# Threshold attention with a SwiGLU layer: the last group's final feed-forward blocks done chunk by chunk, and the two last copies exchanged between VectorE and ScalarE

## The chip, the cores and the metric

The kernel runs on one core of a Trainium2 chip. The metric is device time in microseconds (us). Times are medians of several executions; the profile is one execution, so its span can differ from the median. The kernel before took 564.16 us (564.16 to 564.22, three runs).

## The reference, cut to what matters

```python
def _attn_ref(q, k, v, tau):                 # 8 batches, 8 heads, 576 rows, head size 64
    scores = scale * np.matmul(q, k.transpose(0, 1, 3, 2))
    thresh = np.max(scores, axis=-1, keepdims=True) - tau
    scores = np.where(scores >= thresh, scores, -1000000000.0)
    ...                                      # softmax
    return np.matmul(attn, v)

def _moe_ref(x, w_gate, w_val, w_out, rms_g):  # x: 4608 x 512, feed-forward width 1536
    xn = x / rms * rms_g
    g = xn @ w_gate
    silu = g * (1.0 / (1.0 + np.exp(-g)))
    val = xn @ w_val
    return (silu * val @ w_out).astype(np.float32)
```

Only the last product, `(silu * val) @ w_out`, for the last 256 of 4608 rows, is touched by the change.

## The kernel before

The kernel builds a list of operations, each with an engine, an estimated cost, a priority and the operations that it depends on; a greedy simulation then orders them. Rows go through the feed-forward layer in groups of chunks of 128 rows. The last group has two chunks. The width of 1536 makes twelve blocks of 128. For the last group the output product is "streamed": each block's product is added to the chunk's sums in PSUM as soon as the block's gated values (`hf`) are there.

```python
        if streamed:
            acc = None
            for fc, (hi, m_) in enumerate(hs):          # twelve blocks
                def omm(o, fc=fc, hi=hi, first=acc):
                    for j in range(len(parts)):         # two chunks
                        nc.tensor.matmul(ring[(first or o).slot[j]], hf[hi][:, 128 * j:128 * (j + 1)], wo[:, fc],
                                         start=(fc == 0), stop=(fc == NFC - 1))
                ...
        for j, (ci, _) in enumerate(parts):
            ...
            late = streamed and j % 2
            def ev(o, ...):                             # the copy of a chunk's sums, PSUM to SBUF
                if late:
                    nc.vector.tensor_scalar(out=osb[oi], in0=ring[mo.slot[at]], scalar1=0.5, scalar2=None, op0=ALU.mult)
                else:
                    nc.scalar.activation(out=osb[oi], in_=ring[mo.slot[at]], func=AF.Copy, scale=0.5)
            def store(o, ...):
                    ...
                    (nc.scalar if late else nc.sync).dma_start(out=dst, in_=osb[oi])
```

So chunk 0 is copied by ScalarE and stored from SyncE's queue; chunk 1 is copied by VectorE and stored from ScalarE's queue.

Of the kernel before, what the change touches and what calls it, by code (L numbers as in the profile page):

```python
# [15 lines left out]
COST = dict(  # L16
    s_main=932.0, s_virt=900.0, tr_qk=530.0, tr4=230.0, tr_full=440.0, av_main=310.0, av_virt=480.0, ffn4=216.0, warm=3500.0,
    ttr=690.0, evac_qk=600.0, evac_half=380.0, evac_kt=350.0, prelu=700.0, exp2=1250.0, exp1=690.0, exp0=690.0,
    mask_d=750.0, mask_g=1740.0, take_g=1300.0, trw=510.0, evac_w=450.0, evac_wp=900.0, rz=180.0, xmul=420.0, sq=800.0, xn=720.0,
    pool_tiny=270.0, pool_mean=800.0, pool_dma=850.0, cast_v=650.0, cast_vt=420.0, cast_w=720.0,  # L20
    sp=420.0, sp_v=600.0, sp_w=600.0, sp_tr=1300.0, sp_qk=680.0, sp_tl=630.0,
)
# [105 lines left out]
def kernel(  # L128
# [18 lines left out]
    NFC = DFF // 128  # L147
# [10 lines left out]
    def ps(name, n):  # L158
        return psum.tile([128, n], FP32, tag=name, name=name)
# [49 lines left out]
    ring = [ps(f"ring{i}", 512) for i in range(4)]  # L209
# [11 lines left out]
    def add(eng, cost, prio, deps, fn, **kw):  # L221
        o = Op(eng, cost, prio, deps, fn, **kw)
        ops.append(o)
        return o
# [543 lines left out]
    sl_use, th_use, osb_use = {}, {}, {}  # L768
# [3 lines left out]
    def emit_ffn(slot, parts, ready_step, pace, streamed):  # L772

        n = 128 * len(parts)
        push1 = EPUSH[1] if parts[0][0] < EPUSH[0] else PUSH[1]
        nu = NFC + len(parts)
        st = max(clock[0], ready_step)
        dt = pace * n / 512.0 / nu
        clock[0] = st + pace * n / 512.0
        xops = [t for _, t in parts]  # L780
        hs = []
        mm = 4 * COST["ffn4"] * n / 512.0
        el = (n + 90) / 0.96
        uses = []
        for fc in range(NFC):
            pr = st + dt * fc
            fs = slice(128 * fc, 128 * (fc + 1))
            i = count["gv"] % NT_
            count["gv"] += 1
            hi = count["hf"] % NHF  # L790
            count["hf"] += 1

            def gmm(o, fs=fs):
                for d in range(4):
                    nc.tensor.matmul(ring[o.slot[0]][:, 0:n], wg[d][:, fs], xnT[slot][:, d, 0:n],  # L795
                                     start=(d == 0), stop=(d == 3))

            def vmm(o, fs=fs):
                for d in range(4):
                    nc.tensor.matmul(ring[o.slot[0]][:, 0:n], wv[d][:, fs], xnT[slot][:, d, 0:n],  # L800
                                     start=(d == 0), stop=(d == 3))

            g = add("PE", mm, pr, count["v"] + xops + w_done[fc // 4] + hf_use.get(hi, []), gmm, ring="R")
            vv = add("PE", mm, pr + 0.01, [g] + xops + hf_use.get(hi, []), vmm, ring="R")

            count["v"] = [vv]

            def tanh(o, i=i, g=g):
                nc.scalar.activation(out=th[i][:, 0:n], in_=ring[g.slot[0]][:, 0:n], func=AF.Tanh, scale=0.5)  # L809

            def silu(o, i=i, g=g):
                nc.vector.scalar_tensor_tensor(  # L812
                    out=sl[i][:, 0:n], in0=th[i][:, 0:n], scalar=1.0, in1=ring[g.slot[0]][:, 0:n],
                    op0=ALU.add, op1=ALU.mult)

            def gate(o, i=i, vv=vv, hi=hi):
                nc.vector.tensor_tensor(out=hf[hi][:, 0:n], in0=ring[vv.slot[0]][:, 0:n], in1=sl[i][:, 0:n], op=ALU.mult)  # L817

            t = add("ACT", el, pr - PUSH[0], [g, th_use.get(i)], tanh)
            s_ = add("DVE", el + 40, pr - push1, [t, sl_use.get(i)], silu, frees=(g, 0))  # L820
            th_use[i] = s_
            m_ = add("DVE", el, pr - push1, [s_, vv], gate, frees=(vv, 0))
            sl_use[i] = m_
            hs.append((hi, m_))
            uses += [g, vv]
        xnT_use[slot] = uses
        outs = []
        if streamed:

            acc = None  # L830
            for fc, (hi, m_) in enumerate(hs):
                def omm(o, fc=fc, hi=hi, first=acc):
                    for j in range(len(parts)):
                        nc.tensor.matmul(ring[(first or o).slot[j]], hf[hi][:, 128 * j:128 * (j + 1)], wo[:, fc],  # L834
                                         start=(fc == 0), stop=(fc == NFC - 1))

                mo = add("PE", len(parts) * COST["ffn4"], st + dt * (fc + OUT_LAG), [m_] + wo_ld + outs[-1:], omm,
                         ring=None if acc else "R", nring=len(parts))
                if not acc:

                    acc, mo.pick = mo, ACC
                outs.append(mo)
                hf_use[hi] = [mo]
        for j, (ci, _) in enumerate(parts):
            kind, b, c = chunks[ci]
            pr = st + dt * (NFC + j)
            oi = count["o"] % 2
            count["o"] += 1
            if streamed:
                mo, at = acc, j  # L850
            else:
                mo, at = None, 0
                for lo in range(0, NFC, OUT_PART):
                    def omm(o, j=j, lo=lo, first=mo):
                        for fc in range(lo, lo + OUT_PART):
                            nc.tensor.matmul(ring[(first or o).slot[0]], hf[hs[fc][0]][:, 128 * j:128 * (j + 1)],  # L856
                                             wo[:, fc], start=(fc == 0), stop=(fc == NFC - 1))

                    need = [m_ for _, m_ in hs[0:lo + OUT_PART]] + wo_ld + (outs[-1:] if mo else [])
                    o = add("PE", OUT_PART * COST["ffn4"], pr - (1.0 if mo else 0.0), need, omm, ring=None if mo else "R")  # L860
                    mo = mo or o
                    outs.append(o)

            late = streamed and j % 2

            def ev(o, oi=oi, mo=mo, at=at, late=late):
                if late:
                    nc.vector.tensor_scalar(out=osb[oi], in0=ring[mo.slot[at]], scalar1=0.5, scalar2=None, op0=ALU.mult)
                else:
                    nc.scalar.activation(out=osb[oi], in_=ring[mo.slot[at]], func=AF.Copy, scale=0.5)  # L870

            def store(o, oi=oi, kind=kind, b=b, c=c, late=late):
                if kind == "m":
                    dst = out[b * S:b * S + MAIN].rearrange("(si sc) d -> si sc d", sc=4)[:, c]
                    (nc.scalar if late else nc.sync).dma_start(out=dst, in_=osb[oi])
                else:
                    for e in range(2):
                        r0 = (2 * b + e) * S + MAIN
                        nc.sync.dma_start(out=out[r0:r0 + TAIL], in_=osb[oi][64 * e:64 * e + 64])

            e = add("DVE" if late else "ACT", 690.0 if late else 620.0, pr - PUSH[0], [outs[-1], osb_use.get(oi)], ev,
                    frees=(mo, at))
            late = late and kind == "m"
            osb_use[oi] = add("ACT" if late else "SP", COST["sp"] if kind == "m" else 1100.0, pr, [e], store,
                              dma=DMA_NS['out'])
        if not streamed:
            for hi, _ in hs:
                hf_use[hi] = list(outs)
# [23 lines left out]
    for c in range(DFF // 512):  # L912
        for d in range(0, 4, 2):
            for w_dram, w_sb in ((moe_w_gate, wg), (moe_w_val, wv)):
                slot = n // 2 % len(stage)
                pr = W_FROM + W_STEP * n
# [17 lines left out]
    wo_ld = []  # L934
    wo_src = moe_w_out.rearrange("(fc p) d -> p fc d", p=128)
    for j in range(4):
        o = add("POOL", COST["pool_dma"], W_FROM + W_STEP * n + j + WO_AT, [], lambda o, j=j: nc.gpsimd.dma_start(
            out=wo[:, 3 * j:3 * j + 3], in_=wo_src[:, 3 * j:3 * j + 3]), dma=DMA_NS['wo'], bulk=True)
# [3 lines left out]
    for s, (ci, p) in enumerate(steps):  # L942
# [5 lines left out]
        if p == NP - 1:  # L948
            gi, j = place[ci]
            xt_op[ci] = emit_x(ci, s, gi % NXT, 128 * j)  # L950
            if ci in last_of:
                g = groups[last_of[ci]]
                emit_ffn(last_of[ci] % NXT, [(ci_of[x], xt_op[ci_of[x]]) for x in g], s + (ELAG if place[ci][0] < NELAG else LAG), PACE,
                         last_of[ci] >= len(groups) - STREAMED)
# [19 lines left out]


PACE = 13.0
ACC = (4, 6)
OPENS = ((4,), (6,))
NHF = 12
# [7 lines left out]
OUT_LAG = 5.0  # L987
# [6 lines left out]
PUSH = (40.0, 0.0)  # L994
# [54 lines left out]
```

## Time and profile before

| what | value | where it is read |
|---|---|---|
| median time | 564.16 us | three runs |
| span of the profiled run | 562.9 us | first line of the page |
| TensorE busy | 98% | first part of the page |
| last matmul ends | 558.85 us | timeline, start plus duration of the last row of matmuls |
| last store issued, landed | 559.61, 562.0 us | timeline, and 2.4 us from issue to landing in the DMA view |

TensorE is busy for 98% of the span, and its last matmul ends at 558.85. Four microseconds follow: a copy, a store's issue, its landing and a closing. The lines themselves are in the prediction. One number I call the **tail**: the span less the end of the last matmul, 562.9 - (556.53 + 2.32) = 4.05 us.

### The profile page before, as it was taken

The numbers are of one execution on the slowest core, as the hardware profiler recorded it, in microseconds if no ns is written. First come the engines' busy times: TensorE is split into PE (matmuls) and PEld (weight loads), VectorE is DVE, ScalarE is ACT, GpSimd is POOL, SyncE is SP. The second block draws the span as 40 slices with busy tenths as digits, with TensorE's granted clock in tenths as the row PEclk, the third lists the DMA queues.
The fourth block names the chain that finished last, engine by engine and source line by source line (L and its number), as shares of the span: only waits on it lengthen the run. The fifth ranks groups of instructions, "written<-read, shape, count | busy, mean of one in ns | idle before, by whom it ended". The sixth has DMA issues, their size and how long they took to land.

```text
span 562.9 us, 15217 instructions
## 1 busy us (share of the span) xinstructions
PE 553.0 (98%) x5768; PEld 315.7 (56%) x5768; DVE 425.5 (76%) x1091; ACT 459.9 (82%) x741; POOL 322.5 (57%) x462
## 2 busy tenths in 40 slices
PE   8899999999999999999999999999999999999997
PEld 4656766757767555545555455545555444444674
DVE  4889987869968589658885889578966886596354
ACT  5999998998989788879888997888989988885332
POOL 2378946985767456665667666666666664551000
PEclk9999999999999999999999999999999999999999
DMA  8999999979986498889887799988898544662210
GB/s 189 259 283 271 159 191 192 193 145 187 202 184 115 111 178 156 181 161 186 151 175 174 122 168 179 181 179 157 171 189 178 116 95 92 151 95 52 85 39 37
DMA packets 270025, 89.08 MB, mean 158 GB/s; under 512 B 252544, under 2 KB 262272, under 8 KB 269952
## 3 DMA queue, kind: packets, MB, share of 16 engines
q1 hardware_dynamic: 267168, 86.02, 75.8%
q0 software_dynamic: 1600, 1.57, 1.8%
q8 instruction: 45, 0.74, 0.6%
q10 hardware_dynamic: 1184, 0.52, 0.3%
q14 instruction: 28, 0.23, 0.2%
HBM read 37.75 MB, written 9.44 MB: 84 GB/s over the span
## 4 chain that ended last, share of the span: by engine, by line
PE 94%; DVE 2%; ACT 1%; DMA 1%; issue 1%; POOL 0%; SPq 0%; DVEq 0%
PE s_ps L569 30%; PE ring L795 17%; PE ring L800 16%; PE ring L856 15%; PE ring L700 6%; PE ring L304 2%; PE ring L696 2%; DVE ssb L592 1%; PE ring L662 1%; PE s_ps L800 1%; PE s_ps L834 1%; PE s_ps L856 1%; DMA stage<-in_q_dram 1%; PE ring L365 1%; PE s_ps L795 0%
## 5 line engine op out<-in xcount | busy, mean ns | idle before, releaser
L592 DVE CUSTOM_DVE_ANT_0 ssb<-s_ps,zrow 128x576 f32<-128x576 f32 x288 | 207.1, 752 | 64.4 <-PE s_ps L569 46.5
L610 ACT ACTIVATE ssb<-ssb,nth 128x576 f32<-128x576 f32 x224 | 166.1, 767 | 27.5 <-POOL nth L599 27.1
L569 PE MATMUL s_ps<-qkt 64*64 64x288 f32 (+1 forms) x1792 | 165.9, 417 | 1.5 <-DVE mx L592 1.5
L643 POOL TENSOR_SCALAR wsb<-ssb,nth 128x576 f16<-128x576 f32 x64 | 110.5, 1726 | 9.7 <-DMA wt<-wsb 3.2
L795 PE MATMUL ring<-xnT,wg 128*128 128x256 f16 (+1 forms) x564 | 114.4, 325 | 0.3 <-DVE xsb L718 0.3
L569 PEld LDWEIGHTS s_ps<-qkt 64*64 64x64 f32 (+1 forms) x1792 | 78.1, 140 | 62.5 <-DVE mx L592 15.5
L800 PE MATMUL ring<-xnT,wv 128*128 128x512 f16 (+1 forms) x528 | 110.4, 331 | 0.0
L599 POOL TENSOR_SCALAR nth<-mx 128x2 f32<-128x2 f32 x144 | 31.7, 220 | 128.1 <-DVE mx L592 118.0
L812 DVE SCALAR_TENSOR_TENSOR sl<-th,ring 128x256 f32<-128x256 f32 (+1 forms) x141 | 77.0, 546 | 30.9 <-ACT th L809 29.6
L617 ACT ACTIVATE wsb<-ssb 128x1152 f16<-128x1152 f32 x80 | 93.0, 1162 | 4.3 <-DMA wt<-wsb 2.2
L809 ACT ACTIVATE th<-ring 128x256 f32<-128x256 f32 (+1 forms) x141 | 67.5, 480 | 29.7 <-PE ring L795 24.7
L856 PE MATMUL ring<-wo,hf 128*128 128x512 f16 x384 | 90.0, 380 | 0.0
L648 POOL TENSOR_TENSOR wsb<-wsb,esb 128x576 f16<-128x576 f16 x64 | 81.8, 1279 | 10.3 <-ACT esb L629 6.0
L817 DVE TENSOR_TENSOR hf<-ring,sl 128x512 f16<-128x512 f32 (+1 forms) x132 | 74.9, 567 | 9.3 <-PE ring L800 0.5
L800 PEld LDWEIGHTS <-wv 128*128 128x128 f16 x576 | 52.2, 98 | 44.5 <-issue 14.2
L795 PEld LDWEIGHTS <-wg 128*128 128x128 f16 x576 | 52.0, 98 | 42.2 <-issue 12.2
L856 PEld LDWEIGHTS <-hf 128*128 128x128 f16 x408 | 37.3, 98 | 47.0 <-issue 7.0
L629 ACT ACTIVATE esb<-ssb,nth 128x576 f16<-128x576 f32 x64 | 49.2, 769 | 6.1 <-POOL nth L599 5.8
L700 PE MATMUL ring<-va,wt 128*128 128x65 f16 (+1 forms) x1264 | 53.0, 193 | 0.0
L700 PEld LDWEIGHTS <-wt 128*128 128x128 f16 (+1 forms) x1280 | 48.8, 100 | 3.8 <-issue 0.7
L614 ACT ACTIVATE wsb<-ssb 128x576 f16<-128x576 f32 x64 | 43.6, 681 | 1.6
L696 PE MATMUL ring<-va,wt 128*128 128x130 f16 (+1 forms) x158 | 35.2, 227 | 0.6 <-ACT qTv L473 0.6
(68 smaller groups left out, 442.3 us busy)
## 6 DMA issues: line engine op xcount, KB each, us to landing
vst<-in_v_dram SPq DMA_DIRECT2D x32, 256.0 KB, 3.7
qkn<-in_k_dram SPq DMA_DIRECT2D x31, 256.0 KB, 3.8
out_dram<-osb SPq DMA_DIRECT2D x31, 256.0 KB, 2.8
qkn<-in_q_dram SPq DMA_DIRECT2D x28, 256.0 KB, 4.3
stage<-in_moe_w_gate_dram SPq DMA_DIRECT2D x6, 512.0 KB, 5.9
stage<-in_moe_w_val_dram SPq DMA_DIRECT2D x6, 512.0 KB, 6.5
wt<-wsb SPq DMA_TRANSPOSE x128, 3.3
wo<-in_moe_w_out_dram POOLq DMA_DIRECT2D x4, 384.0 KB, 6.6
```

Source lines behind the costliest of these rows:

```text
L569: nc.tensor.matmul(s_ps[h][rows, ROW_AT + n * part:ROW_AT + n * part + n], lhs(hs), kT[i][p][h][hs, n * part:n * part + n], start=True, st ...
L592: nc.vector.tensor_tensor_reduce(out=ssb[a][:, h], in0=s_ps[h][:, ROW_AT:ROW_AT + S], in1=zrow, scale=-1.0 / 8.0, scalar=3.0e38, op0=ALU.a ...
L610: nc.scalar.activation(out=ssb[a][:, h], in_=ssb[a][:, h], func=PRELU, scale=-1.0, bias=nth[m][:, h:h + 1], **PRELU_KW)
L617: nc.scalar.activation(out=wsb[s % NW], in_=ssb[a], func=AF.Exp)
L643: nc.gpsimd.tensor_scalar(out=wsb[s % NW][:, h], in0=ssb[a][:, h], scalar1=nth[m][:, h:h + 1], scalar2=None, op0=ALU.is_le)
L648: nc.gpsimd.tensor_tensor(out=wsb[s % NW][:, h], in0=wsb[s % NW][:, h], in1=esb[es], op=ALU.mult)
L700: nc.tensor.matmul(ring[o.slot[0]][rs, at:at + D + 1], w[:, 5 * h + j, rs], va[vi][:, p, 2 * j + h], start=False, stop=(h == 1 and j == 3))
L795: nc.tensor.matmul(ring[o.slot[0]][:, 0:n], wg[d][:, fs], xnT[slot][:, d, 0:n], start=(d == 0), stop=(d == 3))
L800: nc.tensor.matmul(ring[o.slot[0]][:, 0:n], wv[d][:, fs], xnT[slot][:, d, 0:n], start=(d == 0), stop=(d == 3))
L812: nc.vector.scalar_tensor_tensor(out=sl[i][:, 0:n], in0=th[i][:, 0:n], scalar=1.0, in1=ring[g.slot[0]][:, 0:n], op0=ALU.add, op1=ALU.mult)
L817: nc.vector.tensor_tensor(out=hf[hi][:, 0:n], in0=ring[vv.slot[0]][:, 0:n], in1=sl[i][:, 0:n], op=ALU.mult)
L856: nc.tensor.matmul(ring[(first or o).slot[0]], hf[hs[fc][0]][:, 128 * j:128 * (j + 1)], wo[:, fc], start=(fc == 0), stop=(fc == NFC - 1))
```

## The change

The intent is to have chunk 0's sums complete earlier, so that its copy and store are out of the way when chunk 1's come, and to let chunk 1's copy and store both be done by ScalarE.

```diff
-            for fc, (hi, m_) in enumerate(hs):
-                def omm(o, fc=fc, hi=hi, first=acc):
-                    for j in range(len(parts)):
+            turns = [(fc, tuple(range(len(parts)))) for fc in range(NFC - BY_ROW)]
+            turns += [(fc, (j,)) for j in range(len(parts)) for fc in range(NFC - BY_ROW, NFC)]
+            last_out = {}
+            for n_, (fc, js) in enumerate(turns):
+                hi, m_ = hs[fc]
+                def omm(o, fc=fc, hi=hi, js=js, first=acc):
+                    for j in js:
                         nc.tensor.matmul(...)
 ...
-                if late:
+                if streamed and not late:
                     nc.vector.tensor_scalar(...)
                 else:
                     nc.scalar.activation(...)
 ...
-            e = add("DVE" if late else "ACT", ..., [outs[-1], osb_use.get(oi)], ev,
+            on_dve = streamed and not late
+            e = add("DVE" if on_dve else "ACT", ..., [last_out[j] if streamed else outs[-1], osb_use.get(oi)], ev,
 ...
+BY_ROW = 4
```

The queues of the stores are not changed: chunk 0 by SyncE, chunk 1 by ScalarE.

More of the change, by code (lines that the diff above doesn't have):

```diff
@@ L830, in emit_ffn @@
             acc = None
-            for fc, (hi, m_) in enumerate(hs):
-                def omm(o, fc=fc, hi=hi, first=acc):
-                    for j in range(len(parts)):
+            turns = [(fc, tuple(range(len(parts)))) for fc in range(NFC - BY_ROW)]
[5 more added lines that the diff above has]
+                    for j in js:
                         nc.tensor.matmul(ring[(first or o).slot[j]], hf[hi][:, 128 * j:128 * (j + 1)], wo[:, fc],
                                          start=(fc == 0), stop=(fc == NFC - 1))
-                mo = add("PE", len(parts) * COST["ffn4"], st + dt * (fc + OUT_LAG), [m_] + wo_ld + outs[-1:], omm,
-                         ring=None if acc else "R", nring=len(parts))
+                late = len(js) == 1 and js[0]
+                mo = add("PE", len(js) * COST["ffn4"], st + dt * (fc + OUT_LAG + (NFC if late else 0)),
+                         [m_] + wo_ld + outs[-1:], omm, ring=None if acc else "R", nring=len(parts))
                 if not acc:
@@ L842, in emit_ffn @@
                 outs.append(mo)
+                for j in js:
+                    last_out[j] = mo
                 hf_use[hi] = [mo]
@@ L879, in store @@
                         nc.sync.dma_start(out=out[r0:r0 + TAIL], in_=osb[oi][64 * e:64 * e + 64])
-            e = add("DVE" if late else "ACT", 690.0 if late else 620.0, pr - PUSH[0], [outs[-1], osb_use.get(oi)], ev,
+            on_dve = streamed and not late
+            e = add("DVE" if on_dve else "ACT", 690.0 if on_dve else 620.0, pr - PUSH[0],
+                    [last_out[j] if streamed else outs[-1], osb_use.get(oi)], ev,
                     frees=(mo, at))
```

## The prediction

> **What bounds the kernel now.** I read the page's header and engine shares first, then the timeline of the last microseconds, since the change touches only the last group's end, then the chain of waits there, and last the DMA view of the same stretch.
>
> ```profile
> span 562.9 us, 15217 instructions
> ...
> PE 553.0 (98%) x5768; PEld 315.7 (56%) x5768; DVE 425.5 (76%) x1091; ACT 459.9 (82%) x741; POOL 322.5 (57%) x462
> ```
>
> TensorE is busy 98% of the span, and the other engines have room. Whatever does not shorten TensorE's stream can gain only in what follows its last matmul. The timeline (start, duration, engine, line, operation) shows that end:
>
> ```profile
> 556.09 0.60 PE L800 MATMUL ring<-xnT,wv 128*128 128x256 f16 x4
> 556.28 0.42 DVE L812 SCALAR_TENSOR_TENSOR sl<-th,ring 128x256 f32<-128x256 f32 x1 [0.36 <-ACT th L809]
> 556.42 1.93 PEld L834 LDWEIGHTS <-hf 128*128 128x128 f16 x10
> 556.53 2.32 PE L834 MATMUL s_ps<-wo,hf 128*128 128x512 f16 x10
> 556.80 0.42 DVE L817 TENSOR_TENSOR hf<-ring,sl 128x256 f16<-128x256 f32 x1
> 558.67 0.60 ACT L870 ACTIVATE osb<-s_ps 128x512 f32<-128x512 f32 x1 [2.43 <-PE s_ps L834]
> 558.89 0.69 DVE L868 TENSOR_SCALAR osb<-s_ps 128x512 f32<-128x512 f32 x1 [1.66 <-PE s_ps L834]
> 559.29 0.33 SPq L875 DMA_DIRECT2D out_dram<-osb  x1
> 559.61 0.36 ACTq L875 DMA_DIRECT2D out_dram<-osb  x1
> ```
>
> The reader is to see three things. The ten last matmuls (blocks 7 to 11 for two chunks) are evenly spaced: (2.32 - 0.379 that one takes) / 9 = 0.216 us. ScalarE copies chunk 0 from 558.67, after the last but one matmul; VectorE copies chunk 1 from 558.89, 0.04 after the last matmul ended (556.53 + 2.32 = 558.85). And the two stores go out 0.32 us apart, so they are on the DMA engines together. The chain that ended last says the same of the last store's origin:
>
> ```profile
> 556.69 2.17 PE s_ps L834 x10
> 558.87 0.02 issue
> 558.89 0.69 DVE osb L868
> ```
>
> The end is matmuls, VectorE's copy of chunk 1, its store, the landing, and the program's closing. The DMA view of 559 to 563 us (40 slices of 0.1 us) shows what the store costs:
>
> ```profile
> DMA  0000000000059999999999999200000000000000
> GB/s 0 0 0 0 0 0 0 0 0 0 0 205 389 430 389 369 389 348 431 389 369 369 389 369 348 62 0 0 0 0 0 0 0 0 0 0 0 0 0 0
> ...
> out_dram<-osb SPq DMA_DIRECT2D x1, 256.0 KB, 2.2
> out_dram<-osb ACTq DMA_DIRECT2D x1, 256.0 KB, 2.4
> ```
>
> From about 560.1 to 561.55 all 16 engines are full: two stores of 256 KB back to back. ScalarE's store lands 2.4 us after its issue, at 559.61 + 2.4 = 562.0; the remaining 0.9 us to 562.9 are the closing, which the change leaves alone. The same kind of store when alone, 541 to 544 us (slices of 0.075 us, issue at 541.26):
>
> ```profile
> DMA  0000000000000036999999963000000000000000
> ```
>
> Its data run from about 542.05 to 542.9, so they begin 0.8 after the issue and take 0.83. The view of the output tensor from 535 to 550 us gives the landing of such lone stores:
>
> ```profile
> DMA to landing us min/median/max: 2.1/2.1/2.1
> ```
>
> So the last store is late by 2.4 - 2.1 = 0.3 us. A second way: alone, it would have had its last byte at 559.61 + 0.8 + 0.83 = 561.25, but the engines fall idle near 561.55, again 0.3.
>
> **What the Trainium skill says.** "DMA: Bandwidth & Descriptors", section "Issuing engines are not separate DMA queues", states that DMAs started by scalar, sync or gpsimd all run on the same 16 DMA engines and interleave. The trace agrees: issued from two queues, 0.52 MB moves at one store's rate, some 390 GB/s. "Perfetto Trace Analysis", section "DMA Instruction — HWDGE (DVE, Sync)", says that the profiled length of the DMA instruction is only the issue. The trace agrees: 0.33 us of issue against 2.1 to landing. "PSUM — Partial Sum Buffer", section "Summary: rules for kernel authors", says to aim at a different bank when PSUM is read while a matmul runs. The two chunks' sums lie in different `s_ps` tiles, and before already copies chunk 0 at 558.67 while the last matmul (558.47 to 558.85) writes the other.
>
> **The change, part by part.**
>
> Order of matmuls. Blocks 0 to 7 stay pairwise; blocks 8 to 11 are then done for chunk 0 (four matmuls) and next for chunk 1 (four). The count stays 24, each with its own weight load, so TensorE's work is the same. Four matmuls in a row into one bank instead of alternating ones should cost nothing: the group before it has runs of 12 into one bank at 2.75 us (L856 in the timeline), and 11 x 0.216 + 0.379 = 2.755. The greedy ordering of the program sees the same candidates up to block 7, so everything before is unchanged. TensorE: 0.
>
> Need for block 11. Chunk 0's block 11 becomes the sixth of the ten instead of the ninth. It would start at 556.53 + 5 x 0.216 = 557.61, its weight load some 0.11 earlier, at 557.50. VectorE writes block 11's `hf` until 556.80 + 0.42 = 557.22. That leaves about 0.28 us. No stall: 0.
>
> Chunk 0's way out. Its last matmul ends at 557.61 + 0.38 = 557.99, four slots of 0.216 before the very last. VectorE starts its copy at 558.03 (0.04 later, as before), ends at 558.72, and SyncE issues the store near 558.75 instead of 559.29: 0.54 earlier. Data run from 559.55 to 560.4. This is off the end's path by itself; it only gets out of the way.
>
> Chunk 1's way out, the path. The last matmul still ends at 558.85, and the copy starts at 558.89. It is ScalarE's now: 0.597 instead of 0.690 (the L870 and L868 rows), ended at 559.49 instead of 559.58: 0.09 gained. The issue follows on ScalarE's own queue. Before, the step from VectorE's end to ScalarE's issue was 0.03, so removing the change of engine can give at most this; and since a write must be complete before a DMA reads it, I expect that a wait of some such size stays. I count 0. The issue is at 559.52. Its data would start at 560.32, with the first store's data ending at 560.4: an overlap of under 0.1 us instead of 0.5. I take the lone store's 2.1: landing at 561.6 instead of 562.0.
>
> Sum: 0.09 (shorter copy) + 0.3 to 0.36 (no queueing behind the other store) = about 0.42 us. 564.16 - 0.42 = 563.74, which is 0.07%.
>
> **The rivals.**
>
> The transfer is late for its queue, not for its neighbour. If a store issued by ScalarE takes 2.4 us even alone, only the copy's 0.09 is gained: 564.07. For it: the profile has no lone store from that queue, and its issue is 0.36 long against 0.33. Against it: the engines are full all through the 1.45 us, and the delay is what sharing would give.
>
> TensorE waits for block 11. If the semaphore from VectorE takes longer than the 0.28 us of slack, every later matmul moves by the difference. Even 0.2 us of it would only halve the gain: 563.95. Against it: elsewhere in this timeline consumers start 0.04 us after producers.
>
> The wait after ScalarE's own copy costs more than one between engines. ScalarE's queue may have to drain before it issues. If this cost 0.3 us, the time would be 564.04. The profile of before has no copy and store on the one queue, so it says nothing against it but that such steps cost 0.03 elsewhere.
>
> The whole order shifts. The order comes from a greedy simulation of all operations; a change early in the list could move microseconds either way. But no earlier operation's cost, priority or dependencies change. I give it about 1%.
>
> **Range and chances.** The central value has all of the removed queueing and the faster copy. If every rival but the last came true together, I would be at about 564.2; if the issue also gains the 0.03 and the landing gets shorter, at 563.6. The runs of before spread by 0.06. So 563.4 to 564.2. The gain or loss would have to be 11 us for a verdict other than the same, which nothing in the last 4 us can give.
>
> **What would show it.** In the changed profile: the L834 row still ten matmuls spaced 0.216 and ending 2.32 after it starts; VectorE's copy at about 558.0 and ScalarE's at 558.9; SyncE's issue 0.5 us earlier; ScalarE's issue within 0.05 after its copy; the DMA view with two humps that hardly overlap; ScalarE's landing 2.1 instead of 2.4; span near 562.5. A gap in the ten matmuls would show the second rival, a landing still of 2.4 with the engines idle before it the first, and a gap between copy and issue the third. A different start of the last group (the first block at 548.7) would show that the order shifted and prove me wrong.

## More of the kernel before

As spans are given to a tenth, a tail is good to about 0.05. The tail has an advantage over the time: what loads do at the start of a run does not enter it. Each tail is read from one profiled execution.

## The result, and the profile after

The changed kernel took 563.88 us (563.40 to 564.06, four runs), the kernel before 564.19 in the same rounds (564.16 to 564.23). The ratio is 0.9993, with a 95% interval from 0.9976 to 1.001. Ratios here are the mean time of one kernel's fast runs over that of the other's in the same rounds, so not quite the ratio of the medians. The time lies in the predicted range, 0.14 us above the predicted 563.74. The interval includes 1, so these times do not show a gain.

The timeline of the changed kernel's end (start us, duration us, engine, line, operation, and in brackets the idle time before and its releaser):

```profile
555.93 2.32 PE L840 MATMUL s_ps<-wo,hf 128*128 128x512 f16 x10
556.21 0.42 DVE L817 TENSOR_TENSOR hf<-ring,sl 128x256 f16<-128x256 f32 x1
557.43 0.69 DVE L877 TENSOR_SCALAR osb<-s_ps 128x512 f32<-128x512 f32 x1 [0.80 <-PE s_ps L840]
558.15 0.33 SPq L884 DMA_DIRECT2D out_dram<-osb  x1
558.29 0.60 ACT L879 ACTIVATE osb<-s_ps 128x512 f32<-128x512 f32 x1 [2.64 <-PE s_ps L840]
558.92 0.36 ACTq L884 DMA_DIRECT2D out_dram<-osb  x1
```

The last matmul ends at 555.93 + 2.32 = 558.25. The ten matmuls take as long as before. Chunk 0's copy now begins 0.82 before that end, and its store is issued 0.10 before it; before, the store was issued 559.29 - 558.85 = 0.44 after it. ScalarE's copy ends at 558.89 and its store is issued 0.03 later. The end of the chain of waits has ScalarE's copy where VectorE's stood:

```profile
556.10 2.17 PE s_ps L840 x10
558.27 0.02 issue
558.29 0.60 ACT osb L879
```

The DMA view of the changed kernel from 558 to 562 us, again in slices of 0.1 us, with the size and the time from issue to landing of each store:

```profile
DMA  0000000003899999629999996100000000000000
GB/s 0 0 0 0 0 0 0 0 0 123 307 369 369 410 430 369 205 82 369 369 369 369 369 451 246 41 0 0 0 0 0 0 0 0 0 0 0 0 0 0
...
out_dram<-osb SPq DMA_DIRECT2D x1, 256.0 KB, 2.1
out_dram<-osb ACTq DMA_DIRECT2D x1, 256.0 KB, 2.1
```

There are two humps with a dip between them instead of one block, and ScalarE's store lands after 2.1 us instead of 2.4. The tail is 561.9 - 558.25 = 3.65 us, 0.40 less than before; the prediction's sum was 0.42.

The span has shrunk by 1.0, though, from 562.9 to 561.9, and 0.6 of this is already there at the last group's first output block (548.71 before, 548.11 after). This part lies before the changed matmuls. In the timeline of the first 24 us, TensorE waits for a load of q in the profiled run of before:

```profile
23.21 0.52 PE L365 MATMUL ring<-id,qkn 128*128 128x128 f32 x3 [0.72 <-DMA qkn<-in_q_dram]
```

In the profiled run of the changed kernel the same transposes start without that wait:

```profile
22.52 0.55 PE L365 MATMUL ring<-id,qkn 128*128 128x128 f32 x3
```

From there on TensorE runs 0.6 ahead to the last group. Whether this differs between kernels or only between executions is a question for the experiments.

### The profile page after: what moved, and what is told of

It reads as the page before. It is cut to its first block, busy times and chain, and to the rows that moved or that the text cites. A ratio compares the mean times of both kernels' runs of the same rounds, so it can differ in the third digit from the quotient of the medians.

```text
span 561.9 us, 15217 instructions
## 1 busy us (share of the span) xinstructions
PE 554.2 (99%) x5768; PEld 316.4 (56%) x5768; DVE 425.3 (76%) x1091; ACT 460.0 (82%) x741; POOL 322.4 (57%) x462
## 4 chain that ended last, share of the span: by engine, by line
PE 95%; DVE 2%; POOL 1%; ACT 1%; issue 1%; DVEq 0%; POOLq 0%
PE s_ps L569 29%; PE ring L795 17%; PE ring L800 16%; PE ring L865 15%; PE ring L700 6%; PE ring L304 2%; PE ring L696 2%; DVE ssb L592 1%; PE ring L662 1%; PE ring L365 1%; PE s_ps L800 1%; PE s_ps L840 1%; PE s_ps L865 1%; PE s_ps L262 1%; PE s_ps L795 0%
```

## The experiments

My theory has two terms: chunk 1's store no longer queues behind chunk 0's on the DMA engines (about 0.3 us), and chunk 1's copy is ScalarE's 0.60 instead of VectorE's 0.69. A first rival says that the gain comes from having copy and store on one engine; a second that ScalarE's queue was slow in itself; a third that the lead of 0.6 belongs to the change. All runs but `small_first`, which is wrong, gave correct results. The tails of all runs are in one table at the end of this section. All times compared here count as fast runs (granted clock 0.996 to 1.0); a run that was executed once has only its tail used.

### changed_again: the changed kernel once more

No edit.

> The changed kernel once more, for the spread. I call tail the span less the end of the last matmul (start plus duration of the last row of matmuls): 562.9 - (556.53 + 2.32) = 4.05 us before, 561.9 - (555.93 + 2.32) = 3.65 changed. Theory (the gain is 0.35 of freed DMA engines plus 0.09 of a shorter copy, all of it after the last matmul): tail 3.65 again, and the time about 0.4 below before's. Rival (the 0.6 us by which the profile already leads at the last group's first block is a gain of the change too): 1.0 below before's, and the lead there in this profile as well.

Measured: 564.26 us median of six (563.97 to 565.93) against 564.86 for the kernel before (564.28 to 565.83, eleven runs of the kernel before in this set); ratio 0.9992, interval 0.998 to 1.0004. The tail is 562.1 - (556.08 + 2.32) = 3.70. The tail agrees with the theory. So does the ratio, 0.0008 of 564.86 being 0.45 us, but its interval includes 1. The lead at the last group was in this profile too (its last matmul ends at 558.40), so by the profile alone the rival could still stand. The times do not rule it out either: 1.0 us below would be a ratio of 0.9982, just inside the interval. The next run settles it.

### order_only: only the matmuls' order

```diff
-                if streamed and not late:
+                if late:
                     nc.vector.tensor_scalar(...)
-            on_dve = streamed and not late
+            on_dve = late
```

> Only the order of the matmuls is changed; chunk 0 is copied by ScalarE and stored by SyncE, chunk 1 copied by VectorE and stored by ScalarE, as before. Theory: the stores no longer meet, landing 2.1 instead of 2.4; VectorE's copy is 0.09 longer than ScalarE's, so tail 3.65 + 0.09 = 3.75, about 0.3 below before. Rival (the gain comes from copy and store being on one engine): tail near 4.05.

Measured: 564.34 us (564.01 to 565.84, five runs), ratio 0.9994, interval 0.9982 to 1.0006. The profiled run was a long one, with a span of 563.7:

```profile
557.60 2.32 PE L840 MATMUL s_ps<-wo,hf 128*128 128x512 f16 x10
```

Its last matmul ends at 557.60 + 2.32 = 559.92, 1.7 us later than in the changed kernel, though the edit leaves TensorE's program as it is. Of this, 1.0 us is one wait for the same load of q, at 22.6 us. So the order of the matmuls does not bring the lead with it, and the third rival falls. The kernel before alone spreads over 1.5 us in this set (564.28 to 565.83), which fits with a difference between executions. The tail is 563.7 - 559.92 = 3.78, as the theory has it. ScalarE's landing is 2.1:

```profile
out_dram<-osb SPq DMA_DIRECT2D x1, 256.0 KB, 2.1
out_dram<-osb ACTq DMA_DIRECT2D x1, 256.0 KB, 2.1
```

Copy and store are here on different engines, as before, and most of the gain is there. The first rival falls.

### swap_only: only the copies' engines

```diff
-BY_ROW = 4
+BY_ROW = 0
```

> Only the copies' engines are swapped; the matmuls stay pairwise as before. Theory: chunk 0's copy by VectorE ends 0.09 later, so its store starts 0.09 later; both stores together keep the DMA engines full, and the last landing is set by the first store's start plus both transfers: tail 4.05 + 0.09 = 4.15, a little slower than before, although the last copy is shorter. Rival (one engine for copy and store, with a shorter copy, is worth something of its own): tail 3.95 or less.

Measured: 565.26 us (564.58 to 565.48, five runs), ratio 1.0001, interval 0.9989 to 1.0013. The matmuls' row is

```profile
556.80 2.32 PE L840 MATMUL s_ps<-wo,hf 128*128 128x512 f16 x10
```

and the tail is 563.3 - (556.80 + 2.32) = 4.18. The chunk 1 copy is the short one, and yet the tail is longer than before. The DMA view of 559 to 563 us:

```profile
DMA  0000000000000009999999999999600000000000
...
out_dram<-osb SPq DMA_DIRECT2D x1, 256.0 KB, 2.2
out_dram<-osb ACTq DMA_DIRECT2D x1, 256.0 KB, 2.6
```

ScalarE's store is issued earlier after the last matmul than before (559.79 - 559.12 = 0.67 against 0.76) but lands 2.6 after its issue instead of 2.4: it pays with queueing what it won with the copy. The last byte is set by when the first store starts, and this one starts 0.1 later, since VectorE copies chunk 0 more slowly. So the two terms of the change do not add: without the order the swap is worth less than nothing, with it about 0.1 by the rounded tails (3.78 - 3.65 or 3.70), 0.06 by the unrounded ones of the last table.

### small_first: the store ahead made small

The kernel before, with one store cut to 16 rows of 128:

```diff
-                    (nc.scalar if late else nc.sync).dma_start(out=dst, in_=osb[oi])
+                    if streamed and not late:
+                        nc.sync.dma_start(out=dst[0:16], in_=osb[oi][0:16])
+                    else:
+                        (nc.scalar if late else nc.sync).dma_start(out=dst, in_=osb[oi])
```

> The kernel before, but chunk 0's last store writes 16 of its 128 rows (the result is wrong on purpose). Matmuls, copies and queues are as before; only the transfer ahead of ScalarE's store shrinks to an eighth. Theory (ScalarE's store waits for DMA engines that chunk 0's store keeps full): its landing falls from 2.4 to 2.1 us and the tail from 4.05 to 3.70. Rival (a store issued by ScalarE takes 2.4 by itself in this order): landing 2.4, tail 4.05.

Measured: one run, 564.72 us. The DMA view of the end:

```profile
out_dram<-osb ACTq DMA_DIRECT2D x1, 256.0 KB, 2.1
out_dram<-osb SPq DMA_DIRECT2D x1, 32.0 KB, 1.6
```

Order, copies and queues are those of before; only the bytes ahead are gone, and ScalarE's landing falls to 2.1. The second rival falls: the queue is not slow in itself. The tail is 562.6 - (556.49 + 2.32) = 3.79, where I had 3.70. By the rounded numbers it fell by 0.26 instead of 0.35 (0.32 by the unrounded ones); the issue is as late as before (559.58 - 558.81 = 0.77), so the whole fall is the landing's.

### two_blocks: half the separation

```diff
-BY_ROW = 4
+BY_ROW = 2
```

> The changed kernel with the last two blocks done chunk by chunk instead of four. Chunk 0's sums are ready 2 x 0.216 later, so its store is issued at 0.33 us after the last matmul instead of 0.11 before it. From swap_only and before, two stores that meet land 2.75 us after the first issue (before: issue 559.29, last landing 559.61 + 2.4 = 562.0). Theory: landing at 0.33 + 2.75 = 3.08 after the last matmul, against 2.77 in the changed kernel: tail 3.65 + 0.3 = 3.95. Rival (any chunk-by-chunk order is enough): 3.65.

Measured: one run, 564.23 us. Tail 562.1 - (555.78 + 2.32) = 4.00, and the landings in the DMA view:

```profile
out_dram<-osb SPq DMA_DIRECT2D x1, 256.0 KB, 2.3
out_dram<-osb ACTq DMA_DIRECT2D x1, 256.0 KB, 2.4
```

With two blocks the stores still meet, and most of the gain is gone. This is the dose to go with the effect: 4.18 with none, 4.00 with two, 3.65 to 3.70 with four. A store occupies the engines for 0.83 us; four blocks put the two issues 558.92 - 558.15 = 0.77 apart, which is almost that. Two put them 558.76 - 558.42 = 0.34 apart.

### both_on_sync: copy and store on different engines

```diff
-                    (nc.scalar if late else nc.sync).dma_start(out=dst, in_=osb[oi])
+                    nc.sync.dma_start(out=dst, in_=osb[oi])
```

and the store's operation is given to SyncE in the list as well.

> The changed kernel, but chunk 1's store is issued by SyncE too, so ScalarE's copy hands over to another engine's queue. The stores are now issued 0.8 us apart, longer than the 0.33 that an issue takes. Theory (one engine for copy and store is worth nothing): issue within 0.05 of ScalarE's copy, tail 3.65 within 0.05. Rival (the hand-over costs): tail 3.75 or more.

Measured: one run, 564.27 us; tail 562.1 - (556.16 + 2.32) = 3.62. SyncE issues the store at 559.14, 0.02 after ScalarE's copy ends (558.52 + 0.60). The hand-over from ScalarE to SyncE costs nothing that can be seen. The part of the change's words that sounds most like a gain, one engine's queue for copy and store, is not where the gain is.

### halves_five and halves_six: two versions meant to beat the change

Chunk 1's copy is cut into two halves of 256 columns, and the first half is stored while the second is copied; chunk 0 is got out of the way still earlier.

```diff
+                elif late:
+                    for i, queue in enumerate((nc.sync, nc.scalar)):
+                        cols = slice(256 * i, 256 * i + 256)
+                        nc.scalar.activation(out=osh[i], in_=ring[mo.slot[at]][:, cols], func=AF.Copy, scale=0.5)
+                        queue.dma_start(out=...[:, c_, cols], in_=osh[i])
 ...
-BY_ROW = 4
+BY_ROW = 5          # halves_six: 6
```

`osh` are two idle buffers of the attention part.

> A version meant to beat the changed kernel: the last five blocks chunk by chunk, and chunk 1's copy in two halves of 256 columns on ScalarE, the first stored by SyncE and the second by ScalarE. Chunk 0's store is issued at 0.32 before the last matmul's end. The second half's copy should end at about 0.04 + 0.6 to 0.7, its store carries 128 KB, 0.41 of transfer instead of 0.83. Theory: landing at the later of 0.70 + 0.03 + 0.83 + 0.41 + 0.42 = 2.4 and -0.32 + 2.75 = 2.43 (engines full from the first store on): tail 3.3, time some 0.35 below the changed kernel. Rival (a store's landing is a fixed 2.1 whatever its size, or rows of 1 KB move slower): tail 3.7. TensorE: block 11 is needed 0.216 earlier, with 0.06 of slack left: the ten matmuls should still take 2.32.

> As halves_five with six blocks chunk by chunk. Chunk 1's block 6 can no longer fill the wait before the last value matmuls, so up to 0.2 us is lost ahead of the end and eleven matmuls are left after it; chunk 0's store is issued at 0.54 before the end. Theory: tail 3.3 as set by the second half's own path (2.4), the same as halves_five, and the first-to-last time of the L840 matmuls up to 0.2 longer than its 10.1: so no better than halves_five, perhaps 0.2 worse. Rival (the first store still sets the landing): tail 3.1.

Measured: halves_five 564.36 us (564.25 to 564.94, five runs) against 564.52 for before, ratio 0.9999, interval 0.9985 to 1.0013. halves_six 565.05 us (564.72 to 565.22), ratio 1.0007, interval 0.9994 to 1.0019. The tails are 562.1 - (555.73 + 2.32) = 4.05 and 563.0 - (556.31 + 2.66) = 4.03. Both of my forecasts of 3.3 missed by 0.7, and the rivals (3.7 and 3.1) missed too. The stores of halves_five in the DMA view:

```profile
out_dram<-osb SPq DMA_DIRECT2D x1, 256.0 KB, 2.1
out_dram<-ssb SPq DMA_DIRECT2D x1, 128.0 KB, 1.9
out_dram<-ssb ACTq DMA_DIRECT2D x1, 128.0 KB, 2.0
```

The last one is issued at 558.78 and lands at about 560.8, which is 2.7 us after the last matmul (558.05) where I had 2.4. The changed kernel has 558.92 + 2.1 - 558.25 = 2.77. So two things have to be explained: the landing hardly came forward, and what follows the landing grew from 3.65 - 2.77 = 0.9 to 4.05 - 2.7 = 1.3. For the second I looked at the closing's line, that is, the last instructions of SyncE's queue. In halves_five (operation, count, shortest/median/longest ns, first and last start):

```profile
L1066 SPq EVENT_SEMAPHORE  x10: 17/28/28, 560.8 to 562.1; - x10
L1066 SPq DRAIN  x3: 7/7/7, 561.3 to 561.6; - x3
```

In the changed kernel:

```profile
L1056 SPq EVENT_SEMAPHORE  x9: 17/28/28, 558.5 to 561.9; - x9
L1056 SPq DRAIN  x3: 7/7/7, 561.1 to 561.4; - x3
```

In halves_five not one of the closing waits is passed before 560.8, the moment of the landing; they then follow each other for half a microsecond before the first drain. In the changed kernel they begin at 558.5 and the drain comes within 0.1 of the landing at 558.92 + 2.1 = 561.0. The closing waits for the semaphores of the DMA transfers one after the other, in a fixed order. A third store moves every later transfer on by one in the turn of semaphores, and the last store got the one that is waited for first. That was the new theory, not yet shown, and the next three runs test it.

halves_six shows besides where the chunk-by-chunk order starts to cost. Its timeline:

```profile
556.31 2.66 PE L841 MATMUL s_ps<-wo,hf 128*128 128x512 f16 x11
...
557.28 1.19 PEld L841 LDWEIGHTS <-hf 128*128 128x128 f16 x7 [0.44 <-DVE hf L818]
```

Eleven matmuls would take 10 x 0.216 + 0.379 = 2.54; they take 2.66, as the weight load waits for block 11's `hf`. With five blocks the load also waits (0.22), but the ten matmuls still take 2.32. Four blocks show no such wait. From the first to the last output matmul halves_six takes 10.27 us against 10.14 in the changed kernel, within the 0.2 that I had allowed.

### one_more_load and seven_more_loads: only the turn of the semaphores

```diff
+    pads = [sb(f"pad{i}", [128, 4]) for i in range(1)]      # seven_more_loads: 7
 ...
+                if pads and not streamed and kind == "m":    # in earlier groups' stores
+                    nc.sync.dma_start(out=pads.pop(), in_=moe_rms_g.rearrange("(c p) -> p c", p=128))
```

> The changed kernel with one extra load of 2 KB (the norm's weights, into a buffer that nobody reads) in the middle of the run. Nothing at the end differs but which DMA semaphore the last two stores get. SyncE's closing waits go through these semaphores in a fixed order, one after the other, some 0.06 us each; in halves_five they began only at the landing (560.8) and took until 561.3, in the changed kernel most were passed by 558.8. Theory (a third store had turned the semaphores on by one, so that the last landing was waited for first, and seven waits more came after it): this kernel's last store gets the first one in the order too, and its tail is 3.65 + 7 x 0.06 = 4.07. Rival (the longer closing belongs to the halves themselves): 3.65.

> As one_more_load with seven extra loads, spread over seven earlier stores. With eight semaphores in turn this is one step back: the last store gets the last but one in the order, and one wait of 0.06 remains after the landing. Theory: tail 3.65 + 0.06 = 3.71. Rival (extra loads lengthen the closing by themselves): 4.07 or more.

Measured: one run each, 565.46 and 564.22 us. One extra load of 2 KB in the middle of the run: tail 563.3 - (556.95 + 2.32) = 4.03. Seven of them: 562.1 - (556.00 + 2.32) = 3.78. In both, ScalarE's store lands 2.1 after its issue, as in the changed kernel. The closing's line with one extra load:

```profile
L1059 SPq EVENT_SEMAPHORE  x9: 17/28/2512, 559.5 to 563.2; - x9
```

One of its waits, the first that concerns a transfer still under way, takes 2512 ns: SyncE stands in it until the landing, and the others follow. The same view cut to 561.9 to 562.46 us, from the landing to just before the first drain, counts seven waits with the long one:

```profile
L1059 SPq EVENT_SEMAPHORE  x7: 28/28/2512, 559.5 to 562.4; - x7
```

With seven extra loads the stretch from 561.05 to 561.25 us, again from the landing to the first drain, has two:

```profile
L1059 SPq EVENT_SEMAPHORE  x2: 28/28/28, 561.1 to 561.2; - x2
```

In the changed kernel the wait that the landing ends is the last before the drain. So six waits follow the landing with one load, one with seven, none without. This shows the theory of the closing; a rival that blames the halves or the mere number of loads has both runs against it. My count was one too high: six waits of 0.06 are 0.36, where I had 7 x 0.06. A single transfer of 2 KB, issued at 93.2 us and waited for by nobody, moved the end by some 0.35 us, nearly as much as the whole change.

### halves_five_turned: the halves with a good turn

The edits of halves_five and of seven_more_loads together.

> halves_five with the seven extra loads, which give its last store the last semaphore in the order. Theory: the closing loses its seven waits, tail 4.06 - 0.42 = 3.64, no better than the changed kernel within 0.05, since halving the copy did not bring the last landing forward as I had thought (2.74 after the last matmul against 2.78). Rival (the landing too was late only because of the waits): tail 3.3.

Measured: 565.27 us (564.31 to 566.92, six runs), ratio 1.0012, interval 0.9991 to 1.0032. Tail 562.5 - (556.51 + 2.32) = 3.67. The closing is back to its short form, and the version is level with the change and not better; the seven loads are in the way of nothing that I could see, but the interval is too wide to tell. The ratio gives no gain over before, although the tail is 0.38 shorter: the six runs spread over 2.6 us, far more than that.

Why the halves do not land earlier is in part my own slip: the two halves go out 0.28 apart (558.50 and 558.78), and on the same engines the second queues behind the first, just as the chunks' stores did. I had reckoned the second half as a lone transfer of 0.41. This is the smaller part. By the DMA views the last bytes of halves_five move at about 560.2, 2.1 after the last matmul, and those of the changed kernel at about 560.55, 2.3 after it: the bytes are 0.2 earlier, but the landing follows them after some 0.6 instead of 0.5, so it gains only some 0.04. A landing is 1.9 to 2.0 us for half the bytes and 2.1 for all of them, and why it shrinks so little no run shows. With the closing set right the tail is close to the 3.7 that the rival of halves_five had named, a landing that does not shrink with the size.

### All tails

| run | time, us | tail, us | tail, unrounded | expected tail |
|---|---|---|---|---|
| before | 564.16 | 4.05 | 4.10 | |
| changed | 563.88 | 3.65 | 3.68 | 3.63 (4.05 - 0.42) |
| changed_again | 564.26 | 3.70 | 3.69 | 3.65 |
| order_only | 564.34 | 3.78 | 3.75 | 3.75 |
| swap_only | 565.26 | 4.18 | 4.20 | 4.15 |
| small_first | 564.72 | 3.79 | 3.78 | 3.70 |
| two_blocks | 564.23 | 4.00 | 3.99 | 3.95 |
| both_on_sync | 564.27 | 3.62 | 3.66 | 3.65 |
| halves_five | 564.36 | 4.05 | 4.06 | 3.3 |
| halves_six | 565.05 | 4.03 | 4.02 | 3.3 |
| one_more_load | 565.46 | 4.03 | 4.03 | 4.07 |
| seven_more_loads | 564.22 | 3.78 | 3.74 | 3.71 |
| halves_five_turned | 565.27 | 3.67 | 3.64 | 3.64 |

The kept traces hold times to the nanosecond, and the column of unrounded tails is worked out from them. There the changed kernel's two profiles agree within 0.01, and its gain is 0.41 to 0.42. The tail of before comes from one profile.

Times of different sets are not to be compared; the median of before was 564.19, 564.86, 564.52 and 564.61 in the four sets. No version that I tried is clearly better than the changed kernel.

## Why the prediction was right

**TensorE unchanged.** Right. The ten matmuls take 2.32, four in a row into one bank cost nothing, and block 11 was in time. The slack of 0.28 that I had worked out holds: one block more uses it up so far that the weight load waits without delay to the matmuls, two more cost 0.12.

**Chunk 0 out of the way.** Right: its copy and its store stand within 0.03 of where I put them relative to the last matmul. That this, and not the engine of the copy, is the larger term is shown by order_only (3.78) against swap_only (4.18), and its mechanism, bytes ahead on the DMA engines, by small_first.

**The shorter copy.** Right in size: 0.60 against 0.69 in the rows, and about 0.1 between order_only's tail and the change's (0.06 unrounded). What I did not say is that it counts only when the stores do not meet: with the pairwise order, the same swap lengthens the tail.

**The issue on ScalarE's own queue.** I counted 0, and the step is 0.03 as before. The third rival, a drain before the issue, falls with that, and both_on_sync shows that the pairing is worth nothing either way.

**The sum.** 0.42 forecast, 0.40 by the tails, 0.39 and 0.45 by the ratios of the two sets (0.0007 x 564.19 and 0.0008 x 564.86). The single ratios' intervals include 1, so the times alone do not show a gain; the tails do. That the median came within 0.14 us of 563.74 is partly luck: in the next set the same kernel's median was 564.26, above my range.

**What I misjudged.** The spread. I took before's 0.06 for the noise of an execution. Over all sets the kernel before ran from 563.85 to 566.95, and the changed kernel from 563.40 to 565.93. Between the profiles of before and of the changed kernel the difference in the start of the last group arises at early waits for loads (0.72 us at 23 us in before's profile, none in the changed kernel's), and not at the end. My line that an earlier start of the last group would prove me wrong was ill chosen for the same reason: the start did move, by 0.6, and between executions of the same TensorE program by up to 1.7. The span near 562.5 failed with it: it was 561.9. The upper end of my range was wrongly summed, too: all rivals but the last together are 564.16 - 0.09 + 0.2 + 0.3 = 564.57, and not about 564.2. And the closing, which I called 0.9 us that the change leaves alone, is not a constant of the kernel: it stayed at 0.9 because the change has as many transfers as before, so that the last store's wait kept its place.

## What to carry to other kernels

When two stores end a kernel, ask when the first one starts to move and whether it has left the DMA engines when the second comes; with two stores of 256 KB the last landing here was the later of the second's own path (2.1 us from its issue) and some 2.7 us from the first's issue. The same sum failed for the halves, so it is not a rule for stores of other sizes. A gain of tenths of a microsecond in a run of 560 is to be read in the tail of the trace, between the last matmul and the end, since the spread ahead of it (up to 1.7 us here) is larger. Before crediting or blaming an edit that adds or removes a transfer, look at which of the closing waits the last landing is met by.

## What the Trainium skill lacked or had wrong

- Closing waits: no page has it that the program's last instructions pass the DMA semaphores in a fixed order, so that the landing of the last store is followed by as many further waits, some 0.06 us each, as stand behind its semaphore. The runs show tails of 3.65 and 3.78 with it last or last but one, and 4.03 to 4.05 with it first.
- "TensorE: Matmul & The Clock Gate", section "Back-to-back issue gap", gives some 131 ns per matmul as the sustained rate of weight load and matmul pairs at 512 columns, and 216 ns as the isolated gap. In this case's streams of such pairs the spacing is 216 ns: ten in 2.32 us with 0.379 for one, and twelve in 2.75 us.
- "DMA: Bandwidth & Descriptors", section "Latency and other measured facts", speaks of a fixed cost of about 2 us for a DMA, smaller where HBM has less to do. Here stores to the output took, from issue to landing, 1.6 us for 32 KB, 1.9 for 128 KB and 2.1 for 256 KB, transfer included.
